# Score matmuls of one unit issued as one operation, column groups in turn, and Wo loaded ahead of V, in a two-layer attention and GLU decode kernel

## Chip, cores and metric

One core of one Trainium2 chip. The metric is the device time of the kernel in microseconds (us), median of several runs; before the change 223.32 us (3 runs, 222.83 to 223.54). A run is called slow when it is over 1.5% above the fastest run of the same kernel.

## The reference, cut to what matters

```python
x = x + A(layernorm(x)); x = x + B(layernorm(x))   # twice
def A(x, k_cache, v_cache, wq, wo):      # 4 batches, 1 query, 32 query heads, 8 K/V heads
    q = x @ wq                           # 512 x 4096
    k, v = caches[:, :, -2048:, :]       # window of 2048 keys, head size 128, bf16
    p = softmax(q k^T / sqrt(128))
    return (p v) @ wo                    # 4096 x 512
def B(x, w_gate, w_up, w_down):          # gated layer, 512 -> 1792 -> 512
    return (sigmoid(x @ w_gate) * (x @ w_up)) @ w_down
```

Both layers use the same weights and caches. The kernel works in two batch groups (batches 0, 1 and 2, 3) so that a group's K and V, once loaded, serve both layers: attention of layer 1 for group 0 ("first attention"), its GLU, then attention of layer 2 for group 0 together with attention of layer 1 for group 1 ("middle attention", two at once), the middle GLU, and attention of layer 2 for group 1 ("last attention") with its GLU.

## The kernel before

The text uses the profile's short names: PE is the matrix engine (TensorE), DVE the vector engine, ACT the scalar engine, DMA the loads. SBUF is the memory that holds the loads (`arena` in the profile), PSUM the one that PE's sums are written to (`ps`). A stage is bound by what its waits end on last.

An attention is four units of four (K/V head, batch) pairs. Each pair writes its scores to its own 32 PSUM partitions; the matmuls that write to the same 32 partitions are called a column group here. A unit's scores fill one PSUM bank. Each pair is one operation of four accumulating matmuls (16 columns of weights, 512 columns streamed):

```python
for gi, (h, b) in enumerate(pairs):
    s = where[("K", h, b)]
    def e_s(pe, gi=gi, s=s, h=h, b=b):
        kt = slot_ap(s).rearrange("p (j c k t) -> p c t j k", c=2, k=32, t=2)
        for cp in range(4):                       # four parts of q
            q0 = ((b * HKV + h) * 4 + cp) * NR
            last = pe.matmul(ps[32 * gi:32 * gi + NR, bank, :], qbd[:, q0:q0 + NR],
                             kt[:, cp // 2, cp % 2, :, :], start=(cp == 0), stop=(cp == 3))
        return last
    P.op("tensor", "S%s_%d_%d" % (tag, h, b), 4 * tm["pe_row"], e_s, ...)
# ... then: max over the bank (DVE), exp (ACT), permutation (PE, "pp"), transpose (DVE),
#     sums (PE, "sb"); PV: 16 small matmuls a pair; Wo: 16 small matmuls a head
```

`P.op` only records an operation, its estimated time and what it depends on. When the kernel is built, a list scheduler orders the operations of each engine; it may put other work between the four score operations of a unit. Loads sit in SBUF slots of 512 KB (49 of them), are issued in a fixed order, and wait until a slot is free. That order is, per unit:

```python
for (h, b) in us[ui + 1]:  load_kv(("K", h, b), A_k, b, h)
for (h, b) in pairs:       load_kv(("V", h, b), A_v, b, h)
add_weights("wo", 2 * gi, [("wo", h) for h in hs])   # Wo is loaded once, for group 0
```

In the first attention each K must also be transposed by DVE before its score matmuls.

## Time and profile before

223.32 us. The profiled run was a slow one (226.36 us; span of the trace 224.6 us). How the time divides, from the timeline:

| stage | ends at us | bound by |
|---|---|---|
| first attention | 70.2 | loads |
| its GLU | 87.1 | loads |
| q, start of the middle attention | 99.7 | loads |
| middle attention (two at once) | 158.5 | PE |
| GLU, reload of Wq, q | 183.0 | PE, then loads |
| last attention | 210.2 | PE and softmax |
| last GLU, output | 224.6 | PE, small steps |

The page's head: PE busy time, then three rows in 40 equal slices, in tenths (PE busy, TensorE clock on record, DMA busy) and GB/s.

```profile
span 224.6 us, 6136 instructions
PE 148.8 (66%) x2796; PEld 97.6 (43%) x2796; DVE 89.8 (40%) x219; ACT 19.4 (9%) x54; POOL 2.8 (1%) x8
PE   1444786739443633736989998998555558999564
PEclk9999995967855555555575579655555558755555
DMA  5999999999999799999999999700099999200000
GB/s 179 354 414 411 408 377 409 386 392 407 384 376 382 243 348 399 279 397 395 400 346 393 414 410 406 297 5 3 0 302 407 411 405 365 88 0 3 0 3 4
```

DMA is busy to slice 25 (141 us), then nearly idle until the middle GLU frees slots; PE is dense in the middle and near the end. The groups of PE instructions: line, operation, shapes and count, busy us, mean ns of one, idle before it.

```profile
L626 PE MATMUL ps<-arena,qbd 128*16 128x512 bf16 x256 | 55.0, 532 | 11.1 <-DVE qbd L591 5.9
L674 PE MATMUL ps<-ebuf,arena 128*128 128x4 bf16 x1024 | 31.2, 165 | 4.0 <-DMA arena<-in_A_v_cache_dram 2.8
L704 PE MATMUL ps<-onb,arena 128*128 128x2 bf16 x512 | 18.4, 165 | 6.5 <-DMA arena<-in_A_wo_dram 5.1
```

L626 are the score matmuls, the costliest group; L674 is PV and L704 is Wo. The timeline of PE in the middle attention: start, duration, operation.

```profile
144.56 1.89 PE L626 MATMUL ps<-arena,qbd 128*16 128x512 bf16 x8
146.38 0.58 PE L704 MATMUL ps<-onb,arena 128*128 128x2 bf16 x16
146.89 1.87 PE L626 MATMUL ps<-arena,qbd 128*16 128x512 bf16 x4
148.70 0.58 PE L704 MATMUL ps<-onb,arena 128*128 128x2 bf16 x16
149.21 1.87 PE L626 MATMUL ps<-arena,qbd 128*16 128x512 bf16 x4
```

This is one unit: two pairs side by side (x8) take 1.89 us, and then each pair left alone takes as long again. The unit lasts 6.5 us because Wo matmuls of another unit stand between its pairs.

### The profile page before, as it was taken

Reading aid. Unit: us, or ns where it says so; the run is one execution under the profiler, and the core shown is the slowest. Engines: PE = TensorE matmul, PEld = TensorE weight load, DVE = VectorE, ACT = ScalarE, POOL = GpSimd, SP = SyncE. Lnnn points to the kernel's source line nnn. Section 1 sums busy time; section 2 is a strip of 40 time slices with the busy share of each in tenths; the row PEclk is TensorE's granted clock in tenths of the full one; section 3 lists DMA queues with packets and bytes.
Section 4 is the critical chain, followed back from the end, with each engine's and each line's share of the span. In section 5 each row is a group of like instructions: output and inputs, shape, how many; then the busy total and the mean of one; then the engine's idle time right before and its main releaser. Section 6 shows DMA issues by size and latency. Waiting matters only on the chain.

```text
span 224.6 us, 6136 instructions
## 1 busy us (share of the span) xinstructions
PE 148.8 (66%) x2796; PEld 97.6 (43%) x2796; DVE 89.8 (40%) x219; ACT 19.4 (9%) x54; POOL 2.8 (1%) x8
## 2 busy tenths in 40 slices
PE   1444786739443633736989998998555558999564
PEld 1341243333433522611286635647454434638453
DVE  4018976537302012288496925403212027404211
ACT  2002020100100000012011002101000012101000
POOL 4000000000000000000000000000000000000000
PEclk9999995967855555555575579655555558755555
DMA  5999999999999799999999999700099999200000
GB/s 179 354 414 411 408 377 409 386 392 407 384 376 382 243 348 399 279 397 395 400 346 393 414 410 406 297 5 3 0 302 407 411 405 365 88 0 3 0 3 4
DMA packets 25386, 65.16 MB, mean 290 GB/s; under 512 B 2056, under 2 KB 11536, under 8 KB 25360
## 3 DMA queue, kind: packets, MB, share of 16 engines
q1 hardware_dynamic: 25360, 64.77, 77.1%
q8 instruction: 22, 0.36, 0.7%
q14 instruction: 4, 0.03, 0.0%
HBM read 64.75 MB, written 0.00 MB: 288 GB/s over the span
## 4 chain that ended last, share of the span: by engine, by line
PE 38%; SPq 24%; DMA 18%; DVE 11%; issue 4%; ACT 4%; ACTq 0%
SPq L364 24%; PE ps L626 16%; DMA arena<-in_A_wo_dram 6%; PE ps L674 5%; DMA arena<-in_A_wq_dram 5%; PE ps L755 4%; PE ps L704 4%; DMA arena<-in_B_w_down_dram 4%; DVE nmax L633 3%; PE ps L646 3%; DMA arena<-in_A_k_cache_dram 3%; ACT prow L642 3%; PE ps L783 2%; DMA arena<-in_B_w_gate_dram 2%; DVE arena L607 2%
## 5 line engine op out<-in xcount | busy, mean ns | idle before, releaser
L626 PE MATMUL ps<-arena,qbd 128*16 128x512 bf16 x256 | 55.0, 532 | 11.1 <-DVE qbd L591 5.9
L607 DVE STREAM_TRANSPOSE arena<-arena 128x1024 f32<-128x1024 f32 x32 | 38.9, 1231 | 12.1 <-DMA arena<-in_A_k_cache_dram 11.8
L674 PE MATMUL ps<-ebuf,arena 128*128 128x4 bf16 x1024 | 31.2, 165 | 4.0 <-DMA arena<-in_A_v_cache_dram 2.8
L674 PEld LDWEIGHTS ps<-ebuf,arena 128*128 128x128 bf16 x1024 | 30.2, 102 | 7.7 <-issue 3.4
L626 PEld LDWEIGHTS ps<-arena,qbd 128*16 128x16 bf16 x256 | 14.2, 104 | 36.9 <-issue 19.5
L704 PEld LDWEIGHTS ps<-onb,arena 128*128 128x128 bf16 x512 | 16.4, 104 | 14.7 <-issue 6.9
L704 PE MATMUL ps<-onb,arena 128*128 128x2 bf16 x512 | 18.4, 165 | 6.5 <-DMA arena<-in_A_wo_dram 5.1
L563 PE MATMUL ps<-xn,arena 128*128 128x2 bf16 (+1 forms) x384 | 13.9, 166 | 12.6 <-DMA arena<-in_A_wq_dram 7.2
L633 DVE TENSOR_REDUCE nmax<-ps 128x1 f32<-128x512 f32 x16 | 11.0, 689 | 22.4 <-PE ps L626 22.3
L642 ACT ACTIVATE prow<-ps,nmax 128x512 bf16<-128x512 f32 x16 | 11.0, 687 | 103.2 <-DVE nmax L639 86.7
L755 PE MATMUL ps<-xn,arena 128*128 128x2 bf16 (+1 forms) x336 | 12.3, 165 | 10.5 <-DVE xn L546 4.2
L563 PEld LDWEIGHTS ps<-xn,arena 128*128 128x128 bf16 x384 | 12.2, 105 | 14.3 <-DMA arena<-in_A_wq_dram 8.1
L755 PEld LDWEIGHTS ps<-xn,arena 128*128 128x128 bf16 x336 | 10.9, 104 | 11.9 <-issue 8.1
L646 PE MATMUL ps<-prow,perm 128*128 128x512 bf16 x16 | 8.0, 498 | 9.2 <-ACT prow L642 9.1
L649 DVE STREAM_TRANSPOSE ebuf<-ps 128x512 f32<-128x512 f32 x16 | 11.3, 709 | 5.7 <-PE ps L646 5.6
L783 PE MATMUL ps<-hT,arena 128*128 128x2 bf16 (+1 forms) x168 | 6.2, 166 | 7.3 <-DVE hT L773 3.8
L783 PEld LDWEIGHTS ps<-hT,arena 128*128 128x128 bf16 x168 | 5.5, 104 | 8.0 <-DMA arena<-in_B_w_down_dram 4.1
L686 DVE TENSOR_TENSOR onb<-ps,rinv 128x16 bf16<-128x16 f32 x16 | 2.6, 161 | 15.0 <-PE ps L674 15.0
L767 DVE TENSOR_SCALAR eg<-eg 128x28 f32<-128x28 f32 (+1 forms) x3 | 0.6, 184 | 19.9 <-ACT eg L764 19.9
L571 DVE TENSOR_SCALAR qT<-ps 128x64 bf16<-128x64 f32 (+1 forms) x3 | 1.6, 519 | 17.3 <-PE ps L563 17.3
L646 PEld LDWEIGHTS ps<-prow,perm 128*128 128x128 bf16 x16 | 1.6, 99 | 14.5 <-ACT prow L642 13.5
L656 PEld LDWEIGHTS ps<-ssel,ones_f 128*128 128x128 f32 x32 | 6.2, 241 | 3.3 <-DVE ssel L653 1.9
(47 smaller groups left out, 59.5 us busy)
## 6 DMA issues: line engine op xcount, KB each, us to landing
arena<-in_A_k_cache_dram SPq DMA_DIRECT2D x32, 512.0 KB, 10.3
arena<-in_A_v_cache_dram SPq DMA_DIRECT2D x32, 512.0 KB, 12.0
arena<-in_A_wq_dram SPq DMA_DIRECT2D x20, 512.0 KB, 7.5
arena<-in_B_w_gate_dram SPq DMA_DIRECT2D x12, 448.0 KB, 10.8
arena<-in_B_w_up_dram SPq DMA_DIRECT2D x12, 448.0 KB, 9.8
arena<-in_B_w_down_dram SPq DMA_DIRECT2D x9, 512.0 KB, 7.5
arena<-in_A_wo_dram SPq DMA_DIRECT2D x8, 512.0 KB, 15.6
arena<-in_B_w_down_dram SPq DMA_DIRECT2D x3, 256.0 KB, 8.0
```

The lines of the kernel that those rows point to most:

```text
L364: o = P.op("sync", name, 0.0, lambda e, dst=dst, src=src: e.dma_start(dst, src), r=r, w=w, dma_bytes=nbytes, dma_rate=tm[rate])
L563: last = pe.matmul(ps[:, CB, q * nb:(q + 1) * nb], src[:, m * 128:(m + 1) * 128], xn[:, c * NB + b0:c * NB + b1], start=(c == 0 and q == 0 ...
L607: P.op("vector", "T%d_%d" % (h, b), c_dve(1024), lambda v, v32=v32: v.transpose(v32, v32), r=[("slot", s)], w=[("slot", s)])
L626: last = pe.matmul(ps[32 * gi:32 * gi + NR, bank, :], qbd[:, q0:q0 + NR], kt[:, cp // 2, cp % 2, :, :], start=(cp == 0), stop=(cp == 3))
L633: lambda v: v.tensor_reduce(nmax[:, k2:k2 + 1], ps[:, bank, :], AXX, ALU.max),
L642: lambda a: a.activation(prow[:, :], ps[:, bank, :], ACTF.Exp, bias=nmax[:, 2 + k2:3 + k2], scale=1.0, accum_out=psm[:, k2:k2 + 1]),
L646: lambda pe: pe.matmul(ps[:, PB, :], perm[:, :], prow[:, :], start=True, stop=True),
L649: lambda v: v.transpose(ebuf[:, k2 * 512:(k2 + 1) * 512], ps[:, PB, :]),
L674: last = pe.matmul(ps[:, ob, gi * REP:(gi + 1) * REP], src[:, j * 128:(j + 1) * 128], ev[:, 1, j, gi * REP:(gi + 1) * REP], start=(j == 0) ...
L704: last = pe.matmul(ps[:, wb, c * nb:(c + 1) * nb], slot_ap(s)[:, r_ * D + c * 128:r_ * D + (c + 1) * 128], ov[:, o0:o0 + nb], start=(h == ...
L755: last = pe.matmul(ps[:, CB, o0 + fc * nb:o0 + (fc + 1) * nb], src[:, fc * 128:(fc + 1) * 128], xn[:, c * NB + b0:c * NB + b1], start=(c = ...
L783: last = pe.matmul(ps[:, CB, 128 + c * nb:128 + (c + 1) * nb], src[:, (fc - a) * D + c * 128:(fc - a) * D + (c + 1) * 128], hT[:, fc * nb: ...
```

## The change

The intent: column groups that stand together run at once (in the trace of the kernel before, at 99.66 us, the 32 matmuls of two units take 3.63 us, where the four of one pair alone take 1.87), so all 16 matmuls of a unit become one operation that cannot be cut apart, and the groups take turns in it. Wo moves ahead of V in the queue, so that V comes last.

```diff
-            for gi, (h, b) in enumerate(pairs):
-                s = where[("K", h, b)]
-                def e_s(pe, gi=gi, s=s, h=h, b=b):
-                    kt = slot_ap(s).rearrange(...)
-                    for cp in range(4):
+            ks = [where[("K", h, b)] for (h, b) in pairs]
+            def e_s(pe):
+                for cp in range(4):
+                    for gi, (h, b) in enumerate(pairs):
+                        kt = slot_ap(ks[gi]).rearrange(...)
                         last = pe.matmul(ps[32 * gi:32 * gi + NR, bank, :], ...)   # as before
-                P.op("tensor", "S%s_%d_%d" % (tag, h, b), 4 * tm["pe_row"], e_s, ...)
+            P.op("tensor", "S" + tag, 16 * tm["pe_row"], e_s, ...)
@@ queue
+                hs = set(h for h, b in pairs)
+                add_weights("wo", 2 * gi, [("wo", h) for h in hs])
                 for (h, b) in pairs:
                     load_kv(("V", h, b), A_v, b, h)
-                hs = set(h for h, b in pairs)
-                add_weights("wo", 2 * gi, [("wo", h) for h in hs])
```

More of the change, by code (lines that the diff above doesn't have):

```diff
@@ L617, in softmax_unit @@
             ob = OBS[k2]
-            for gi, (h, b) in enumerate(pairs):
-                s = where[("K", h, b)]
-                def e_s(pe, gi=gi, s=s, h=h, b=b):
-                    last = None
-                    kt = slot_ap(s).rearrange("p (j c k t) -> p c t j k", c=2, k=32, t=2)
-                    for cp in range(4):
+            ks = [where[("K", h, b)] for (h, b) in pairs]
+            def e_s(pe):
+                last = None
+                for cp in range(4):
+                    for gi, (h, b) in enumerate(pairs):
+                        kt = slot_ap(ks[gi]).rearrange("p (j c k t) -> p c t j k", c=2, k=32, t=2)
                         q0 = ((b * HKV + h) * 4 + cp) * NR
@@ L627, in e_s @@
                                          kt[:, cp // 2, cp % 2, :, :], start=(cp == 0), stop=(cp == 3))
-                    return last
-                P.op("tensor", "S%s_%d_%d" % (tag, h, b), 4 * tm["pe_row"], e_s,
-                     r=[("slot", s)] + [("q", b, a) for a in range(4)], w=[("pss", k2, gi)], banks=(bank,))
+                return last
+            P.op("tensor", "S" + tag, 16 * tm["pe_row"], e_s,
+                 r=[("slot", s) for s in ks] + [("q", b, a) for (h, b) in pairs for a in range(4)],
+                 w=[("pss", k2)], banks=(bank,))
             mk = mxt[:, k2 * 32:(k2 + 1) * 32]
@@ L633, in softmax_unit @@
                  lambda v: v.tensor_reduce(nmax[:, k2:k2 + 1], ps[:, bank, :], AXX, ALU.max),
-                 r=[("pss", k2, gi) for gi in range(4)], w=[("mx", k2)], banks=(bank,))
+                 r=[("pss", k2)], w=[("mx", k2)], banks=(bank,))
             P.op("vector", "mk" + tag, tm["dve_small"],
@@ L643, in softmax_unit @@
                                         accum_out=psm[:, k2:k2 + 1]),
-                 r=[("pss", k2, gi) for gi in range(4)] + [("nm", k2)], w=[("prow",), ("psm", k2)], banks=(bank,))
+                 r=[("pss", k2)] + [("nm", k2)], w=[("prow",), ("psm", k2)], banks=(bank,))
             P.op("tensor", "pp" + tag, tm["pe_sq"],
```

## The prediction

> **What bounds the kernel now.** Windows view: DMA is busy 89 to 104% from 0 to 141 us, then idle (3 to 77 GB/s) except between 161 and 190 us. PE is busy 96% from 107 to 122 us, 88% from 141 to 160 and 85% from 193 to 212, nearly all at half the clock. The chain of waits is DMA queue and landings until 97 us, then PE with softmax between to 158.5 us (end of two attentions), a rigid piece (layer norm, GLU, reload of Wq, q) to 183, and the last attention, PE again, to 210.6.
>
> **What the score matmuls cost.** Group L626: 256 matmuls, 55.0 us busy (15.8% of the chain). In the trace, inside one column group, starts are 427 ns apart at half clock (216 at full), so an operation of four alone takes 1.81 us. Where the four operations of a unit stand together (99.66 and 183.03 us) they already run side by side: starts 13 to 17 ns apart, 32 matmuls in 3.63 us. [...] So I expect taking turns inside a unit to be worth almost nothing; what pays is that one operation of 16 can no longer be cut apart by PV, Wo and permutation matmuls.
>
> **Cut-apart units, from the timeline.** 99 to 158 us: 8 units, about 24 us of score time (3.6, then 1.8 + 1.8 + 1.5 + 1.9, then about 13.3 in nine pieces). At 1.85 us a unit at half clock: 14.8. Gain 9. Last attention: units 2 and 3 take 1.1 + 1.1 + 1.8 + 1.8 + 1.8; then about 1.0 + 1.85. Gain 4.7. Before 70 us, units are stretched by the K transposes (1.23 us each) and DMA, and the last key's four matmuls take as long as 16 side by side: no gain.
>
> **What is given back.** Wo before V (only the first group loads Wo): now the last Wo lands and one piece of Wo matmuls (0.6 us) ends the attention at 70.2. With V last, PV (0.6), normalisation (0.4) and Wo (1.3) follow the last landing: +1.6 us; the GLU gates DMA by its releases, so the loads slip too. The softmax chain gets less cover: I allow 1 to 2 us. [...]
>
> **Sum.** -9 + 1.6 + 1.2 to the end of the middle attention (about 152 us), -4.7 in the last: 223.3 - 10.9, or about **212.5 us**, 8 in 10 between 207 and 219. Faster by over 2%: 0.90; within 2%: 0.08; slower: 0.02.
>
> **What would show it.** Score matmuls: the 16 of a unit end within about 1.9 us (half clock) or 1.0 (full) everywhere; end of first attention near 72 us; GLU of the middle starts near 155 instead of 161 us; last attention about 23 us instead of 27.6. Wrong if: the new program order delays a unit until all four K are transposed and PE stalls behind it; the middle stretch turns out to be bound by K and V landings (V ends near 131 us); or the new PE order loses elsewhere.

The sum is complete: 223.3 - 9 + 1.6 + 1.2 - 4.7 = 212.4, given as about 212.5 us; the 1.2 us lies within the 1 to 2 us allowed for the softmax chain. The expectation that taking turns is worth almost nothing rests on the 13 to 17 ns between starts (13 to 21 over all 32 at 99.66 us) where operations stand together group by group. In the three stretches that it puts nearly all at half clock, the clock on record is 0.61, 0.54 and 0.52.

## More of the kernel before

The windows view for score matmuls alone (stretch, its length, PE busy time and count, ..., clock on record, DMA share, GB/s), middle and last attention:

```profile
99.60:158.50 58.90, 25.45 (x128) 6.32 (x128) 0.00 (x0) 0.00 (x0) 0.00 (x0) 0.62 0.78 303
183.00:210.20 27.20, 11.41 (x64) 3.00 (x64) 0.00 (x0) 0.00 (x0) 0.00 (x0) 0.63 0.37 129
```

## The result, and the profile after

214.67 us (median of 4 runs, 213.80 to 215.32) against 223.43 us for the kernel before (4 runs): ratio 0.9607, 95% interval 0.9565 to 0.9649, so 3.9% faster. A ratio here is the mean time of one kernel's fast runs over that of the other's of the same rounds, so not quite the ratio of the medians. The profiled run was fast (215.32 us, span 213.5).

```profile
span 213.5 us, 6140 instructions
PE 124.1 (58%) x2796; PEld 91.4 (43%) x2796; DVE 89.1 (42%) x219; ACT 19.4 (9%) x54; POOL 2.8 (1%) x8
PE   1441345452563543473698969785554649998564
PEclk9999999999999999999976557855555555555555
L626 PE MATMUL ps<-arena,qbd 128*16 128x512 bf16 x256 | 28.4, 584 | 21.6 <-DVE arena L607 17.1
```

The score matmuls went from 55.0 to 28.4 us busy, with a longer mean of one (584 ns): they did not get quicker, they overlap. The clock row needs care. It shows 9 up to slice 20 mainly because the record of this trace has no entry before 103 us; the starts inside a column group at 24 and 54 us are 385 to 427 ns apart. In the kernel before, whose record begins at 23 us, they are 216 ns apart at 29 us, where it shows full clock, and 427 ns at 106 us, where it shows half. So it was half clock here, and the higher mean clock on record (0.773 against 0.65) is no gain.

Score matmuls in the windows of the middle and last attention:

```profile
99.70:150.20 50.50, 13.48 (x128) 3.31 (x128) 0.00 (x0) 0.00 (x0) 0.00 (x0) 0.67 0.91 360
175.60:199.10 23.50, 7.36 (x64) 1.85 (x64) 0.00 (x0) 0.00 (x0) 0.00 (x0) 0.50 0.39 137
```

In the middle attention they fell by 12.0 us, in the last by 4.1. The middle became 8.4 us shorter, not 12. (The second pair of profiles, taken later, agrees: 59.1 us with 25.3 us of score matmuls before, 51.4 us with 14.3 us after.) All PE work in the same window, before and then after:

```profile
99.60:158.50 58.90, 52.85 (x920) 31.60 (x920) 32.36 (x70) 6.22 (x16) 0.00 (x0) 0.62 0.78 303
```

```profile
99.70:150.20 50.50, 40.13 (x920) 27.65 (x920) 32.06 (x71) 6.22 (x16) 0.00 (x0) 0.67 0.91 360
```

PE was idle 6.1 us of it (58.90 - 52.85), and now is 10.4 us (50.50 - 40.13). The chain of waits of this window says what grew; its first line, shares of the window, before and after:

```profile
by line: PE ps L626 40.9%; PE ps L674 13.2%; PE ps L704 9.3%; PE ps L646 7.3%; ACT prow L642 7.2%; DVE nmax L633 7.1%; issue 3.4%; PE ps L656 3.3%; DVE mxt L636 2.3%; DVE arena L607 2.0%; DVE nmax L639 1.7%; DVE ebuf L649 1.2%; DVE rinv L66
```

```profile
by line: PE ps L675 19.3%; DMA arena<-in_A_k_cache_dram 16.9%; PE ps L626 16.6%; issue 14.7%; PE ps L705 12.4%; DVE arena L607 11.5%; DVE nmax L634 5.3%; PE ps L657 4.0%; PE ps L647 3.7%; DVE ebuf L650 2.4%; ACT prow L643 2.1%; DVE mxt L637
```

Score matmuls were 41% of the chain and are 17%. "issue", time in which an engine waited for nothing that the profile shows, rose from 3.4% to 14.7% (2.0 to 7.4 us). The timeline of PE after, at two of these places:

```profile
121.31 0.99 PE L675 MATMUL ps<-ebuf,arena 128*128 128x4 bf16 x32
122.23 0.59 PE L626 MATMUL ps<-arena,qbd 128*16 128x512 bf16 x1
124.71 0.60 PE L626 MATMUL ps<-arena,qbd 128*16 128x512 bf16 x4 [1.88 <-issue]
...
143.59 0.19 PE L705 MATMUL ps<-onb,arena 128*128 128x2 bf16 x2
146.32 0.53 PE L705 MATMUL ps<-onb,arena 128*128 128x2 bf16 x14 [2.54 <-issue]
```

PE stops for 1.88 us after the first matmul of a unit, and for 2.54 us after 2 of the 16 matmuls of a Wo operation. Inside an operation there is no wait for another engine. The trace has five such stops: 1.88, 1.80 and 2.54 us in the middle attention, 1.29 and 1.97 us between it and the last; the first profile of before has none, its second (below) one of 1.25 us.

The end of the first attention, before and after:

```profile
68.09 0.59 PE L704 MATMUL ps<-onb,arena 128*128 128x2 bf16 x16 [0.92 <-DMA arena<-in_A_wo_dram]
69.58 0.59 PE L704 MATMUL ps<-onb,arena 128*128 128x2 bf16 x16 [0.90 <-DMA arena<-in_A_wo_dram]
70.20 0.17 DVE L738 TENSOR_TENSOR xT<-ps,xT 128x8 f32<-128x8 f32 x1 [2.82 <-PE ps L704]
```

```profile
69.30 0.59 PE L675 MATMUL ps<-ebuf,arena 128*128 128x4 bf16 x16 [0.69 <-DMA arena<-in_A_v_cache_dram]
69.92 0.17 DVE L687 TENSOR_TENSOR onb<-ps,rinv 128x16 bf16<-128x16 f32 x1 [7.89 <-PE ps L675]
70.24 0.57 PE L705 MATMUL ps<-onb,arena 128*128 128x2 bf16 x16 [0.36 <-DVE onb L687]
70.96 0.56 PE L705 MATMUL ps<-onb,arena 128*128 128x2 bf16 x16
71.56 0.17 DVE L739 TENSOR_TENSOR xT<-ps,xT 128x8 f32<-128x8 f32 x1 [1.46 <-PE ps L705]
```

The last load lands at the same time, but now PV, the normalisation and the Wo matmuls of the unit's two heads follow it.

### The profile page after: what moved, and what is told of

It is laid out like the page before. It is cut to its first block, busy times and chain, and to the rows that moved or that the text cites. A ratio compares the mean times of both kernels' runs of the same rounds, so it can differ in the third digit from the quotient of the medians.

```text
span 213.5 us, 6140 instructions
## 1 busy us (share of the span) xinstructions
PE 124.1 (58%) x2796; PEld 91.4 (43%) x2796; DVE 89.1 (42%) x219; ACT 19.4 (9%) x54; POOL 2.8 (1%) x8
## 4 chain that ended last, share of the span: by engine, by line
PE 31%; SPq 26%; DMA 19%; DVE 12%; issue 8%; ACT 3%; ACTq 0%
SPq L364 26%; PE ps L675 7%; PE ps L626 7%; DMA arena<-in_A_v_cache_dram 5%; PE ps L705 5%; PE ps L756 5%; DMA arena<-in_A_wq_dram 4%; DMA arena<-in_A_k_cache_dram 4%; DMA arena<-in_B_w_down_dram 3%; DVE arena L607 3%; DMA arena<-in_B_w_gate_dram 2%; DVE nmax L634 2%; PE ps L563 2%; PE ps L647 2%; ACT prow L643 2%
## 5 line engine op out<-in xcount | busy, mean ns | idle before, releaser
L607 DVE STREAM_TRANSPOSE arena<-arena 128x1024 f32<-128x1024 f32 x32 | 39.0, 1232 | 10.3 <-DMA arena<-in_A_k_cache_dram 10.1
L626 PE MATMUL ps<-arena,qbd 128*16 128x512 bf16 x256 | 28.4, 584 | 21.6 <-DVE arena L607 17.1
L675 PE MATMUL ps<-ebuf,arena 128*128 128x4 bf16 x1024 | 32.5, 166 | 10.8 <-DMA arena<-in_A_v_cache_dram 8.1
L675 PEld LDWEIGHTS ps<-ebuf,arena 128*128 128x128 bf16 x1024 | 31.4, 104 | 14.5 <-DMA arena<-in_A_v_cache_dram 10.6
L626 PEld LDWEIGHTS ps<-arena,qbd 128*16 128x16 bf16 x256 | 6.8, 109 | 34.4 <-issue 19.4
L756 PE MATMUL ps<-xn,arena 128*128 128x2 bf16 (+1 forms) x336 | 12.3, 165 | 10.1 <-DVE xn L546 4.2
L756 PEld LDWEIGHTS ps<-xn,arena 128*128 128x128 bf16 x336 | 10.9, 104 | 11.5 <-issue 8.1
L634 DVE TENSOR_REDUCE nmax<-ps 128x1 f32<-128x512 f32 x16 | 10.9, 685 | 11.9 <-PE ps L626 11.8
L647 PE MATMUL ps<-prow,perm 128*128 128x512 bf16 x16 | 8.8, 547 | 4.8 <-ACT prow L643 4.7
L657 PEld LDWEIGHTS ps<-ssel,ones_f 128*128 128x128 f32 x32 | 7.3, 275 | 3.7 <-DVE ssel L654 1.5
L657 PE MATMUL ps<-ssel,ones_f 128*128 128x16 f32 x32 | 7.8, 321 | 0.0
```

What stands on the lines that cost most here:

```text
L607: P.op("vector", "T%d_%d" % (h, b), c_dve(1024), lambda v, v32=v32: v.transpose(v32, v32), r=[("slot", s)], w=[("slot", s)])
L634: lambda v: v.tensor_reduce(nmax[:, k2:k2 + 1], ps[:, bank, :], AXX, ALU.max),
L647: lambda pe: pe.matmul(ps[:, PB, :], perm[:, :], prow[:, :], start=True, stop=True),
L657: lambda pe: pe.matmul(ps[:, ob, 128:128 + NR], ones_f[:, :], sv, start=True, stop=True),
L675: last = pe.matmul(ps[:, ob, gi * REP:(gi + 1) * REP], src[:, j * 128:(j + 1) * 128], ev[:, 1, j, gi * REP:(gi + 1) * REP], start=(j == 0) ...
L756: last = pe.matmul(ps[:, CB, o0 + fc * nb:o0 + (fc + 1) * nb], src[:, fc * 128:(fc + 1) * 128], xn[:, c * NB + b0:c * NB + b1], start=(c = ...
```

## The experiments

Theory: what pays is that a unit's 16 matmuls stand together; the turn-taking itself is worth nothing, the new queue order costs a little, and PE now sometimes waits for its own instructions. Rivals: turn-taking is needed; the queue order pays; the new order of operations pays, not the overlap; the stops belong to certain matmuls or data. "Before" below is the kernel before, run in the same rounds. All eleven runs gave correct results.

| run | us (median) | ratio to before, 95% interval |
|---|---|---|
| the change, again | 214.14 | 0.9598 (0.9545 to 0.9651) |
| merge only | 211.89; again 212.47 | 0.9539 (0.9493 to 0.9584); 0.9528 (0.9485 to 0.9572) |
| queue order only | 225.52 | 1.0070 (0.9997 to 1.0144) |
| pairs outside | 213.54 | 0.9609 (0.9560 to 0.9657) |
| groups kept apart | 254.11 | one run, before 222.72 |
| merge only, 64 PE instructions in front | 213.12 | 0.9547 (0.9477 to 0.9617) |
| the same, 128 | 211.43 | 0.9463 (0.9393 to 0.9533) |
| the same, 192 | 210.88; again 210.66 (one of six slow) | 0.9471 (0.9376 to 0.9567); 0.9448 (0.9396 to 0.9500) |

### Merge without the queue order (merge_only, merge_again), and the change again

```diff
 # the change, with the queue order of before
+                for (h, b) in pairs:
+                    load_kv(("V", h, b), A_v, b, h)
                 hs = set(h for h, b in pairs)
                 add_weights("wo", 2 * gi, [("wo", h) for h in hs])
-                for (h, b) in pairs:
-                    load_kv(("V", h, b), A_v, b, h)
```

> The change without its queue order (V before Wo, as in the kernel before); score matmuls in one operation, in turn. My theory: the merge brings all of the gain and the queue order costs a little, so this takes 213 to 214.5 us, 0 to 1.5 us less than the whole change (214.7), with the first attention ending near 70.2 instead of 71.6 us. Rival (the queue order brings part of the gain): 216 us or more.

> The whole change again, on the same chip as the next two, to compare it with merge only. My theory: 213.5 to 215 us, 1 to 2.5 us above merge only; first attention ends near 71.7 us against 70.0.

> Merge without the queue order, again: 211 to 213 us, and the interval of its ratio to before lies below the whole change's. Rival (the earlier difference was luck of chip and clock): the two agree within 0.3%.

Merge only took 211.89 us, 1.1 us less than the lower edge of what was expected, and 212.47 us in the second call, beside 214.14 us for the whole change on the same chip. The intervals of the two ratios overlap a little (upper edge 0.9572, lower edge 0.9545), so the demand that they lie apart was not met; but on different chips, merge only is 0.7% below the version with the new queue order (0.9539 against 0.9609 with pairs outside, then 0.9528 against 0.9598). Compared directly, six runs against six, the means are 212.34 and 213.96 us, 1.6 us apart. The first attention ends as in the kernel before, on one piece of Wo:

```profile
69.24 0.59 PE L705 MATMUL ps<-onb,arena 128*128 128x2 bf16 x16 [0.87 <-DMA arena<-in_A_wo_dram]
69.86 0.17 DVE L739 TENSOR_TENSOR xT<-ps,xT 128x8 f32<-128x8 f32 x1 [2.73 <-PE ps L705]
```

This is 1.7 us ahead of the whole change (71.56); the first GLU ends 2.0 us ahead (85.97 against 87.97), in the second pair 0.9 us (87.03 against 87.96). At the first score matmul of the middle attention 1.1 and 1.0 us are left (98.7 against 99.8 us, 99.1 against 100.1 us).

### Queue order alone (queue_only)

```diff
 # the kernel before
+                hs = set(h for h, b in pairs)
+                add_weights("wo", 2 * gi, [("wo", h) for h in hs])
                 for (h, b) in pairs:
                     load_kv(("V", h, b), A_v, b, h)
-                hs = set(h for h, b in pairs)
-                add_weights("wo", 2 * gi, [("wo", h) for h in hs])
```

> The kernel before with the new queue order alone (K, Wo, V). My theory: 0 to 1.5 us slower than the kernel before (223.4), so 223.4 to 225 us; first attention ends near 71.6 us instead of 70.2, the first GLU 0.7 to 1.5 us later. Rival (the queue order brings part of the gain): 222 us or less.

The median is 225.52 us, above what was expected, but three of its six runs are slow. The fast runs give 1.0070 with an interval that touches 1. No gain is in sight, and the size agrees with the 0.7% above; alone it would be inconclusive. The trace, of a slow run, has the first attention finished at 71.6 us (end of the addition to x), against 70.4 and 69.9 in the two profiles of before.

### Pairs outside, parts of q inside (pair_outside)

```diff
-                for cp in range(4):
-                    for gi, (h, b) in enumerate(pairs):
+                for gi, (h, b) in enumerate(pairs):
+                    for cp in range(4):
```

> The whole change, but inside the one operation the pairs are outside and the parts of q inside: four matmuls of a column group, then four of the next. Program order of all other work is the same. My theory (the array takes matmuls of other column groups ahead by itself): the same time as the change within 0.5% (213.6 to 215.7), 16 matmuls still end in about 1.9 us at half clock. Rival (matmuls start strictly in program order, so turn-taking is needed): a unit takes 6 us or more and the time is above 225 us.

213.54 us and a ratio of 0.9609, that of the change: the turn-taking is worth nothing that shows. Single starts of the first unit of the last attention, in us (each row is a bunch of four):

```
pairs outside (program order: four of pair 0, four of pair 1, ...)
174.268 174.282 174.300 174.312
174.653 174.673 174.687 174.707
175.080 175.100 175.113 175.133
175.507 175.527 175.540 175.560
the change (program order: one of each pair, then the next part of q)
175.685 175.689 175.692 175.695
176.069 176.084 176.084 176.089
176.496 176.510 176.510 176.516
176.923 176.937 176.937 176.943
```

Four groups start within 44 and 10 ns and go on in step. With pairs outside, the second matmul of the program belongs to the same group as the first and has to wait some 400 ns, yet matmuls later in the program start within 14 to 44 ns. So, in this trace, matmuls of another column group start ahead of one that waits. No record says which matmul of the program it is; this follows from the times, because four of one group alone start 391 to 427 ns apart (before, at 106.0 us), so four that start within 44 ns belong to four groups, and in strict order a unit would take more than 5 us instead of 1.92 (an estimate: twelve waits of some 0.4 us and the last matmul).

### The kernel before, again (before_again)

> The kernel before, unchanged, for a profile in the fast state, because the profiled run of before was slow (226.4 against 223.4 us). Expected: 222.5 to 224 us if the state is fast. If the clock explains the slow state, the parts that differ from the first profile are score matmuls at full clock; if it is PE waiting in the middle of an operation for its next instructions, stalls of 1 to 3 us appear or vanish.

224.39 us, a little above what was expected and 1.8% above the fastest run of before in that call (220.39), so its state is unknown and there is no surely fast profile of before. In the rounds of the experiments the kernel before spread from 220.4 to 225.6 us (29 runs, fast and slow). The two profiles bear out neither explanation offered: the second has a clock on record of 0.648 like the first (0.65), and one stop of 1.25 us where the slower first had none. But over the 29 runs the slower ones do have the lower clock on record (correlation -0.70; 0.632 to 0.650 in the eight slowest, 0.651 to 0.675 in the eight fastest), so the clock is not ruled out, and the cause stays open. Both profiles are slower than the median run, so their stages overstate what it takes, and the gains per stage below add up to more than the 8.8 us of the ratio.

### Groups kept apart (serial)

```diff
 # pairs outside, and ahead of each pair:
+                    pe.matmul(ps[:, CB, 511:512], ident_b[:, :], ident_b[:, 0:1], start=False, stop=True,
+                              skip_group_check=True)
```

One matmul with weights of 128 x 128, one column wide, into a corner of PSUM that nothing reads. The order of all other operations is that of the change on every engine.

> The whole change with pairs outside, and one matmul of the full array (one column, into an unused corner of PSUM) before each column group, so that groups can no longer overlap; the order of all other work is the same. My theory (overlap pays, not the new order of operations): a unit's 16 matmuls take 6.9 us at half or 3.5 to 4 us at full clock instead of 1.9 and 1.0; the middle and last attentions, bound by PE, become 16 to 40 us longer, and the time is 230 to 260 us, above the kernel before, which had part of the overlap by chance. Rival (the new order of operations pays): it stays below 220 us.

254.11 us. The score matmuls of the middle and last attention:

```profile
108.70:178.50 69.80, 36.90 (x128) 9.13 (x128) 0.00 (x0) 0.00 (x0) 0.00 (x0) 0.79 0.68 261
201.90:237.90 36.00, 19.87 (x64) 4.76 (x64) 0.00 (x0) 0.00 (x0) 0.00 (x0) 0.78 0.30 107
```

A unit takes 4.6 us in the middle attention (36.9 / 8), mostly at full clock. With the new order of operations but without overlap, the scores take 36.9 us where the change takes 13.5 and the kernel before 25.5. The separating matmuls are part of this, some 6 us by an estimate: between two groups the starts are 416 or 675 ns apart, within one 216 or 427, about 0.2 us more, 32 times. Without them it would still be above both. So the overlap pays, and the kernel before had a good part of it by chance, wherever the scheduler left pairs of one unit next to each other.

### Where PE stops: instructions in front (m_shift64, m_shift128, m_shift192, m_shift192b)

If PE stops because its next instructions have not arrived, the stops sit at fixed counts of instructions. Counting PE's records in the trace in order of start (weight loads, matmuls, semaphore waits), every stop over 0.3 us inside an operation:

| trace | records ahead of each stop (us it lasts) | sum, us |
|---|---|---|
| before, before again | none; 4289 (1.25) | 0; 1.3 |
| the change | 2753 (1.88), 3265 (1.80), 3521 (2.54), 4033 (1.29), 4289 (1.97) | 9.5 |
| merge only | 2753 (1.91), 3265 (1.76), 3521 (1.71), 4033 (0.74), 4289 (1.70) | 7.8 |
| pairs outside | 2753 (1.91), 3265 (1.84), 3521 (1.44), 4289 (1.52), 4801 (0.76) | 7.5 |
| groups kept apart | 2753 (2.04) | 2.0 |
| queue order only | 4289 (1.90) | 1.9 |
| 64 in front | 2753 (2.43), 3521 (1.72), 4801 (1.60) | 5.8 |
| 128 in front | 2753 (2.33), 3521 (0.86), 3777 (0.99) | 4.2 |
| 192 in front | 2497 (0.42), 2753 (1.96), 3009 (0.66), 3521 (1.12) | 4.2 |

Every one of these counts is 193 above a multiple of 256. The page of the change lists DMA queues; one of them is this (kind, packets, MB, share):

```profile
q8 instruction: 22, 0.36, 0.7%
```

At each stop of the change a 16,384-byte packet of this queue begins between 2.4 us before the stop and 0.1 us after its start (122.38, 137.04, 143.90, 158.11, 169.47 us), and PE goes on 1.3 to 1.6 us after the packet has ended. From the start of the packet to PE's next matmul that is 2.3 to 3.7 us, 1.0 to 2.1 us of it the packet itself; the packet started 3.1 to 7.7 us after PE had passed the count 256 records earlier. The traces bear the pairing out: in the order of time, one such packet belongs to each stretch of 256 records, and of 275 boundaries between such stretches in the 13 traces PE passes none earlier than 2.28 us after the start of the packet in the stretch ahead of it; at the 45 stops it goes on 2.3 to 2.6 us after that start (once 3.7). To test it, idle matmuls went into the first q projection, where PE waits for Wq:

```diff
 # merge only; in the operations of the first q projection, after each piece of Wq
 # (cut: ident_b is added to what the operation reads)
+                        if k == 0:
+                            for _ in range(4):      # 8 and 12 for 128 and 192 instructions
+                                pe.matmul(ps[:, PB, 0:1], ident_b[:, :], ident_b[:, 0:1], start=True, stop=True)
```

> Merge without the queue order, plus 32 idle matmuls of one column (64 PE instructions) in the first q projection, where PE waits for Wq anyway. Theory: PE stands still in the middle of an operation because its next 256 instructions have not arrived, so the stalls sit at fixed counts of PE instructions; with 64 more in front, each stall moves to 64 instructions earlier in the program, and where the work there is slower the stall shrinks or goes: the sum of stalls (7.8 us in merge only) changes by 2 us or more, the time with it (within 207 to 214 us). Rival (the stalls belong to these matmuls or their data): stalls stay at the same matmuls of the program, the time stays at 211.9.

> As the 64 shift, with 64 idle matmuls (128 PE instructions, half of 256). Theory: stalls move by 128 instructions; those at dense runs of small matmuls stay long (1.5 to 2.5 us), those that now fall before score matmuls or waits go. Rival: nothing moves, 211.9 us.

> As the 64 shift, with 96 idle matmuls (192 PE instructions). Theory: stalls move by 192 instructions, a different sum again; the best of the three shifts and of merge only should differ from the worst by 2 us or more. Rival: nothing moves, 211.9 us.

> Merge without the queue order, with 192 PE instructions in front, again: the best seen. If the shorter stalls count, 210.3 to 211.5 us, about 1 us below merge only; if not, within 0.3% of it.

The stops stayed at the same counts and so moved in the program. The stop at 2753 records fell after the first score matmul of a unit in merge only; with 192 in front it falls into a PV operation:

```profile
116.85 0.94 PE L678 MATMUL ps<-ebuf,arena 128*128 128x4 bf16 x30
119.76 0.53 PE L678 MATMUL ps<-ebuf,arena 128*128 128x4 bf16 x14 [1.97 <-issue]
```

So the stops belong to the count of instructions, not to certain matmuls. Their sum fell from 7.8 to 4.2 us; the time fell by less, and not in step with the sum: 64 in front has a smaller sum than merge only but took 213.12 us. In its trace a stop of 1.60 us lies in the last attention, where little hides it. With 192 in front the time is 210.66 us against 212.47 for merge only on the same chip and in the same rounds (ratios 0.9448 and 0.9528; the intervals overlap a little, upper edge 0.9500 and lower edge 0.9485). The expectation, 210.3 to 211.5 us, was met. That is the best version seen, 5.5% below the kernel before and 3.5 us below the change. The best of the three shifts and merge only was expected to differ from the worst by 2 us or more; 210.88 against 213.12 just meets it. That the smaller stops are what makes 192 in front faster is likely and not shown: no run has the idle matmuls without moving the stops. In the second call the sums were 5.8 us with 192 in front and 10.1 us for merge only (8.2 us for the change), so the stops also vary from run to run, but the order is the same.

## Why the prediction was right, point by point

- **Score matmuls overlap when they stand together, and turn-taking is worth nothing: right.** Pairs outside gives the same ratio, and groups kept apart gives 254 us. A unit's 16 matmuls end within 1.9 us at half clock and 1.04 to 1.14 us at full clock (merge only, pairs outside).
- **Gain of 9 us in the middle attention: too small.** The score matmuls fell by 12.0 us (25.45 to 13.48), because before they were 25.5 us and not about 24, and because two and a half of the eight units after still ran at full clock (starts inside a group 206 to 239 ns apart at 105.7, 130.5 and 132.0 us), where the estimate took 1.85 us for each.
- **Given back in the middle, 1.2 us for softmax with less cover: the wrong term.** What grew is PE standing still for instructions, 1.88 + 1.80 + 2.54 = 6.2 us. The window closes with it: score time -12.0, other PE work -0.8 (27.4 to 26.7), stops +6.2, other idle time -1.9 (6.1 to 4.2), in all -8.4 us, as measured (58.90 to 50.50). The prediction said -9 + 1.2 = -7.8. Two mis-sized terms nearly cancelled. The middle GLU, forecast near 155 us, began at 152.9 (161.2 before).
- **Wo before V costs 1.6 us: right.** It measured 1.4 us at the end of the first attention (70.20 to 71.56), 1.7 us against merge only, and 0.7% of the time in two comparisons.
- **The stretch from the middle GLU to the last attention is rigid: not quite.** It went from 24.5 to 25.4 us with stops of 1.29 and 1.97 us in it; in merge only, with shorter stops there, it is 24.7 us. How much of the stops hid behind the landing of Wq is not known.
- **The last attention, about 23 us: right** (175.7 to 199.1, 23.4 us; a gain of 3.8 us where 4.7 was forecast). The unit that was to take 1.0 us at full clock took 1.88 us. Why is not shown: with the same bursts the unit took 1.04 us in merge only (attention 21.6 us) and 1.09 us in the second profile of the change itself (21.9 us). The clock there differs from run to run.
- **Sum.** Predicted -10.9 us, measured -8.8 us (3.93% of 223.43), inside the range of 207 to 219. The missing 2 us are less than the stops of the change, but no run takes all stops away, so how much of the 9.5 us is on the critical path stays open; the version that moved them by 192 is 1.8 us faster than the one it was made from. The missing 2 us can have another source as well: from profile to profile the span fell by 11.1 us (224.6 to 213.5), about what was predicted, but the prediction read its gains from a run that was 3 us slower than the median.

What stays open too: why the packet of a stretch of 256 records starts in time at some boundaries and only when PE has run out at others. That PE simply runs faster now is not enough. From 3265 to 3521 records PE takes 4.3 us after the change (139.4 to 143.8) and 8.4 us before it (146.4 to 154.7), but with the groups kept apart it takes 4.1 us and does not stop at 3521. What differs is when the packet starts. In all nine traces with the merge and the overlap, loads keep DMA fully busy when PE passes 3265 (share 1.03), the packet starts 3.0 to 4.5 us after that, and PE stops at 3521. In the other four traces DMA is nearly idle then (under 9% within 0.5 us), the packet starts within 0.3 us of it, and PE does not stop. So the loads seem to delay the fetch, and the change has moved dense PE work into the time of the loads. No run varies the loads alone, so this is argued and not shown.

## What to carry to other kernels

Before you rely on a clever issue order inside an engine's queue, ask whether the trace shows the work already overlapping when it merely stands together (here 16 matmuls of four column groups took 1.9 us, as long as the four of one group); then the thing to protect is adjacency, by making it one operation for the scheduler. When a change makes a dense instruction stream faster, look in the trace for stops inside an operation: they can be the engine's own instruction fetch (here every one sat 193 above a multiple of 256 records, and in the profile of the change a packet of the instruction queue began between 2.4 us before it and 0.1 us after its start), and moving the boundary by some idle instructions (64 to 192 here) where the engine waits anyway is cheap to try. Test each half of a double change alone: here the smaller half cost 0.7%, and leaving it out beat the whole.
